# Attention in turns of six units instead of three, each turn followed at once by its own products with v

## The chip, the cores and the metric

The kernel runs on one core of a Trainium2 chip. The metric is the time of one execution on the device in microseconds, as the median of several runs. A core has a matrix engine (TensorE, "PE" in the profile; its weight loads are a row of their own, "PEld"), a vector engine (VectorE, "DVE"), a scalar engine with activation functions (ScalarE, "ACT"), a general engine (GpSimd, "POOL") and a queue engine (SyncE, "SP"). The matrix engine writes to PSUM, which here is used as eight banks of 128 partitions x 512 float32. The engines run their own instruction streams in order and wait for one another through semaphores.

## The reference

What is computed, cut to what matters. Queries and keys are each put into the cluster whose centroid they are closest to; a query attends only to keys of its own cluster. Then comes a mixture of experts, where each row goes to one expert.

```python
# q, k, v: (4 batches, 8 heads, 768 rows, 64); centroids: (8, 16, 64)
q_assign = np.argmax(einsum('bhsd,hcd->bhsc', q_n, c_n), axis=-1)     # q_n, k_n, c_n: normed
k_assign = np.argmax(einsum('bhsd,hcd->bhsc', k_n, c_n), axis=-1)
mask = q_assign[:, :, :, None] == k_assign[:, :, None, :]
scores = where(mask, q @ k.T / 8, -1e9)
attn = softmax(scores)                 # exp, divided by its sum + 1e-9
x = (attn @ v) as (3072 rows, 512)
# experts: 8, x (3072, 512), w1 (8, 512, 1024), w2 (8, 1024, 512)
expert_idx = argmax(x @ w_gate); gate_w = the softmax probability of that expert
out[row] = gate_w[row] * (relu(x[row] @ w1[e]) @ w2[e])
```

## The kernel before

Attention works on 16 groups of two heads of one batch. A group has 12 units: two halves of the queries (384 each) by six blocks of 128 keys. There are thus 192 units. One unit is scored in `score`: for each of the two heads a float32 matmul of keys by queries, then a bf16 matmul that adds the mask (a one-hot product, made so that another cluster's score becomes hugely negative). The result, two banks of PSUM ("sps"), is put through the exponential by ACT into an SBUF tile A, and DVE adds A to a running sum T. `attend` multiplies A by v and collects six units in one bank O.

```python
NB = 3                                  # units of a turn
ps_s = tile_pool(name="ps_s", bufs=NB, space=PSUM)      # three double banks "sps"
ps_o = tile_pool(name="ps_o", bufs=1, space=PSUM)       # one bank  "O"
ps_m = tile_pool(name="ps_m", bufs=1, space=PSUM)       # one bank  "mps"
def wide(): return ps_s.tile([P, 2, 512], F32, name="sps")
ap = tile_pool(name="ap", bufs=2 * NB)                  # the tiles A

def score(u):
    g, half, j = where(u)
    ps = ps_s.tile([P, 2, 512], F32, name="sps")
    for a in range(2):                                  # L673, contraction over 64 rows
        nc.tensor.matmul(ps[:, a, 0:HS], lhsT=qk[g][r, 1, ks], rhs=qk[g][r, 0, qs], start=True, stop=False)
    for a in range(2):                                  # L676, the mask
        nc.tensor.matmul(ps[:, a, 0:HS], lhsT=ohT[g][r, 1, ks], rhs=ohT[g][r, 0, qs], start=False, stop=True)
    nc.scalar.activation(A[u], ps[:, :, 0:HS], AF.Exp)  # L678
    # L681 (j == 1) and L685 (j > 1): T[g, half] += A[u] on DVE

def attend(u):                                          # L693, output of 64 partitions per head
    for a in range(2):
        nc.tensor.matmul(O[g, half][a * D : (a + 1) * D, 0:HS], lhsT=rows[g, "v"][:, a, j, :], rhs=a_[:, a, :], ...)
```

Everything else of the attention is cut into jobs that are placed between scores and products. `turn` transposes q and k of a later group (L599; DVE copies one part with the scale at L603, ACT the rest at L604 and L606). `similar` and `similar2` multiply them by the centroids and transpose the result (L613, L624). `assign` and `assign2` find the closest centroid (DVE L632, L633, POOL L634, DVE L640, L641), and `put` transposes the one-hot rows (L651; ACT L655 and DVE L656 copy them to ohT). After a group, `finish` copies O (ACT L701), `weigh` and `weigh2` make the sums and the gate's logits (L711, L725, then five small DVE operations from L727), and `x_turn` transposes the outputs (L754) and scales them on DVE (L757).

```python
def similar(g):
    ps = ps_m.tile([P, 512], F32, name="mps")
    ...                                                 # four matmuls, L613
    nc.scalar.copy(sims[g], ps[:, 0:HS])                # L618
def similar2(g):
    ps = ps_m.tile([P, 512], F32, name="mps")
    ...                                                 # three transposes, L624
    nc.scalar.copy(sims[g], ps[:, 0:HS]...)             # L626

for n in range(-4, NTURN + 5):
    for x in range(n * NB, (n + 1) * NB):               # the scores of this turn's units
        score(x)
    for f, a in jobs.get((n, 0), ()): f(*a)             # jobs, first part
    for x in range((n - 1) * NB, n * NB):               # the products of the turn before
        attend(x)
    for f, a in jobs.get((n, 1), ()): f(*a)             # jobs, second part
```

`gate` and `keep_rows` close a batch (every fourth group); `choose`, `count`, `slots1`, `one_hots1` and `tokens1` sort the first three batches' rows by expert during the last batch's attention. The experts' two layers follow (L301, L345) with gathers and scattered writes on POOL (L270, L316).

Of the kernel before, what the change touches and what calls it, by code (L numbers as in the profile page):

```python
# [8 lines left out]
F32 = mybir.dt.float32  # L9
# [5 lines left out]
PSUM = bass.MemoryType.PSUM  # L15
# [2 lines left out]


BIG = float(2**60)  # L20
NB = 3
XU = 2
RQ = 32
NP = 3
# [159 lines left out]
def kernel(  # L184
# [11 lines left out]
    nc = tc.nc  # L196
    B, H, S, D = q.shape
    C = centroids.shape[1]
    P = 128
    NQ = S // P  # L200
    HP = H // 2
    NG = B * HP
    HS = S // 2
# [6 lines left out]
    FB = F // P  # L210
# [19 lines left out]
    def fetch(e, i):  # L230
        i %= 3
        w1 = wpools[i].tile([P, DB, F], F32, name=f"w1_{i}")
        w2 = wpools[i].tile([P, FB, Dm], F32, name=f"w2_{i}")
        nc.sync.dma_start(out=w1, in_=moe_w1[bass.ds(e, 1)].rearrange("e (a p) f -> p (e a) f", p=P))
        nc.sync.dma_start(out=w2, in_=moe_w2[bass.ds(e, 1)].rearrange("e (a p) d -> p (e a) d", p=P))
        return w1, w2
# [20 lines left out]

    late = ExitStack()
    p1 = late.enter_context(tc.tile_pool(name="first", bufs=2))
    ps_s = late.enter_context(tc.tile_pool(name="ps_s", bufs=NB, space=PSUM))  # L260
    ps_o = late.enter_context(tc.tile_pool(name="ps_o", bufs=1, space=PSUM))
    ps_m = late.enter_context(tc.tile_pool(name="ps_m", bufs=1, space=PSUM))


    def wide():
        return ps_s.tile([P, 2, 512], F32, name="sps")
# [88 lines left out]
    def cols_of(t, c0):  # L355
        return lambda j: t[:, c0 + j : c0 + j + 1]
# [125 lines left out]
    def indices(pool, ps, w, gi, si):  # L482
# [14 lines left out]
            n=[P], rows=NF * P, e=e, gi=cols_of(g_idx1, e), si=cols_of(s_idx1, e), apart=True, scalar_only=True  # L497
# [5 lines left out]
    with ExitStack() as actx:  # L503
# [1 line left out]
        qkp = actx.enter_context(tc.tile_pool(name="qkp", bufs=2))  # L505
        ohp = actx.enter_context(tc.tile_pool(name="ohp", bufs=2))
        asg = actx.enter_context(tc.tile_pool(name="asg", bufs=2))
        ap = actx.enter_context(tc.tile_pool(name="ap", bufs=2 * NB))
        tp_ = actx.enter_context(tc.tile_pool(name="tsum", bufs=2))
        stat = actx.enter_context(tc.tile_pool(name="stat", bufs=2))  # L510
        xp = actx.enter_context(tc.tile_pool(name="xp", bufs=1))
# [1 line left out]
        pl = actx.enter_context(tc.tile_pool(name="places1", bufs=1))  # L513
# [75 lines left out]
        qk, sims, ohT = {}, {}, {}  # L589
# [17 lines left out]

        def similar(g):

            ps = ps_m.tile([P, 512], F32, name="mps")  # L610
            for t in range(4):
                w, half = divmod(t, 2)
                nc.tensor.matmul(  # L613
                    ps[t * 2 * C : (t + 1) * 2 * C, 0:HS], lhsT=cblk[:, g % HP].rearrange("p a c -> p (a c)"),
                    rhs=qk[g][:, w, half * HS : (half + 1) * HS], start=True, stop=True,
                )
            sims[g] = asg.tile([P, HS], F32, name="simT", bufs=1)
            nc.scalar.copy(sims[g], ps[:, 0:HS])  # L618

        def similar2(g):  # L620
            simT = sims.pop(g)
            ps = ps_m.tile([P, 512], F32, name="mps")
            for i in range(NQ // 2):
                nc.tensor.transpose(ps[:, i * P : (i + 1) * P], simT[:, i * P : (i + 1) * P], ident)  # L624
            sims[g] = asg.tile([P, G, C], F32, name="sim")
            nc.scalar.copy(sims[g], ps[:, 0:HS].rearrange("p (t c) -> p t c", c=C))  # L626
# [32 lines left out]
        A, T, O = {}, {}, {}  # L659
        X, XT = {}, {}  # L660

        def where(u):
            g, r = divmod(u, 2 * NQ)
            return g, r // NQ, r % NQ

        def score(u):
            g, half, j = where(u)
            qs = slice(half * HS, (half + 1) * HS)
            ks = slice(j * P, (j + 1) * P)
            ps = ps_s.tile([P, 2, 512], F32, name="sps")  # L670
            for a in range(2):
                r = slice(a * D, (a + 1) * D)
                nc.tensor.matmul(ps[:, a, 0:HS], lhsT=qk[g][r, 1, ks], rhs=qk[g][r, 0, qs], start=True, stop=False)  # L673
            for a in range(2):
                r = slice(a * D, (a + 1) * D)
                nc.tensor.matmul(ps[:, a, 0:HS], lhsT=ohT[g][r, 1, ks], rhs=ohT[g][r, 0, qs], start=False, stop=True)  # L676
            A[u] = ap.tile([P, 2, HS], F32, name="A")
            nc.scalar.activation(A[u], ps[:, :, 0:HS], AF.Exp)  # L678
            if j == 1:
                T[g, half] = tp_.tile([P, 2, HS], F32, name="T", bufs=4)  # L680
                nc.vector.scalar_tensor_tensor(  # L681
                    T[g, half], in0=A[u - 1], scalar=1e-9 / P, in1=A[u], op0=ALU.add, op1=ALU.add
                )
            elif j > 1:
                nc.vector.tensor_tensor(T[g, half], T[g, half], A[u], op=ALU.add)  # L685

        def attend(u):
            g, half, j = where(u)
            if j == 0:
                O[g, half] = ps_o.tile([P, 512], F32, name="O")  # L690
            a_ = A.pop(u)
            for a in range(2):
                nc.tensor.matmul(  # L693
                    O[g, half][a * D : (a + 1) * D, 0:HS], lhsT=rows[g, "v"][:, a, j, :], rhs=a_[:, a, :],
                    start=(j == 0), stop=(j == NQ - 1),
                )
# [89 lines left out]
        def at(n, part, f, *a):  # L786
            jobs.setdefault((n, part), []).append((f, a))

        UG = 2 * NQ
        NU = NG * UG  # L790
        TG = UG // NB
        TH = NQ // NB
        NTURN = NG * TG
        at(1, 1, place_consts)
        for g in range(NG):
            n = g * TG
            if g == 1:

                for f, a in ((turn, (g, 0)), (turn, (g, 1)), (similar, (g,)), (similar2, (g,))):
                    at(-1 if f is similar2 else -2, 1, f, *a)  # L800
            else:
                at(n - 4, 0, turn, g, 0)
                at(n - 4, 1, turn, g, 1)
                at(n - 3, 0, similar, g)
                at(n - 3, 1, similar2, g)
            at(n - 2, 0, assign, g)
            at(n - 2, 0, assign2, g)
            at(n - 1, 0, put, g)
            at(n + TH, 1, finish, g, 0)
            at(n + 2 * TH, 1, finish, g, 1)  # L810
            if g < NG - 1:
                at(n + TG + 2, 0, weigh, g)
                at(n + TG + 2, 1, weigh2, g)
                at(n + TG + 3, 1, x_turn, g, 0)
                at(n + TG + 4, 0, x_turn, g, 1)
                if g % HP == HP - 1:
                    at(n + TG + 3, 0, gate, g // HP)
                    at(n + TG + 4, 0, keep_rows, g // HP)


        front = parts[0]
# [35 lines left out]
            layer1(g, (f0, f1))  # L857

        n = (NG - HP) * TG
        at(n + 3, 1, choose, pl, front)  # L860
        at(n + 4, 1, count, front)
        at(n + 5, 0, slots1)
        at(n + 5, 1, one_hots1, 0)
        at(n + 6, 0, one_hots1, 1)
        at(n + 7, 0, tokens1)
        for i in range(NP):
            at(n + 7, 1, gather1, i)
            at(n + 13, i % 2, turn_rows1, i)

        n = NG * TG  # L870
        at(n + 1, 0, first_half, 0, 0, FB // 4)
        at(n + 1, 0, weigh, NG - 1)
        at(n + 1, 0, first_half, 0, FB // 4, FB // 2)
        at(n + 1, 0, weigh2, NG - 1)
        at(n + 1, 0, x_turn, NG - 1, 0)
        at(n + 1, 1, x_turn, NG - 1, 1)
        at(n + 1, 1, gate, B - 1)
        at(n + 1, 1, keep_rows, B - 1)
        at(n + 2, 0, first_half, 0, FB // 2, FB)
        for g in range(2, NG):  # L880
            at((g - 2) * TG + 1, 0, load, g)

        def early(e):
            weights[e] = fetch(e, e)

        for e in range(2):
            at(HP * TG * (e + 1) - 7, 0, early, e)

        for n in range(-4, NTURN + 5):
            for x in range(n * NB, (n + 1) * NB):  # L890
                if 0 <= x < NU:
                    score(x)
            for f, a in jobs.get((n, 0), ()):
                f(*a)
            for x in range((n - 1) * NB, n * NB):
                if 0 <= x < NU:
                    attend(x)
            for f, a in jobs.get((n, 1), ()):
                f(*a)
# [5 lines left out]
    with tc.tile_pool(name="sm", bufs=1) as sm:  # L905
        front, back = parts
# [20 lines left out]
        for part in parts:  # L927
            n, over = part["n"], part["over"]
# [85 lines left out]
    with tc.If(nx > XU):  # L1014
        with tc.For_i(XU, nx, 1) as i:
# [4 lines left out]
            g = dict(n=[P], rows=N, w=fetch(ex, 0), gi=lambda j: gi[:, 0:1], si=lambda j: gi[:, 1:2], apart=False)  # L1020
# [36 lines left out]
```

## Time and profile before

| | before |
|---|---|
| time, median of 3 runs (lowest to highest) | 864.28 us (863.96 to 864.37) |
| span of the profiled execution | 862.4 us |
| mean granted TensorE clock | 0.993 of full |
| PE / PEld / DVE / ACT / POOL busy | 97% / 50% / 36% / 31% / 12% |
| HBM read and written | 68.26 MB, 13.68 MB |
| first score to last product with v | 21.95 to 428.91 us |

The profile's page gives busy shares of each engine, then the span in 40 equal slices with a digit for tenths of busy time, then groups of instructions: source line, engine, operation, the tiles written and read, count, busy time, mean duration in ns, and the idle time of the engine just before them with what ended it. The timeline lists instructions in order of time, with neighbours of the same line merged: start, duration, engine, line, operation, form, count. A float32 matmul of the program stands as two records. The form shows the part of the array in use: 64*128 is 64 rows of contraction by 128 columns of output.

### The profile page before, as it was taken

The page shows a single profiled execution, that of the slowest core. Times are in us where ns is not written, and L with a number is a line of the kernel's source. Part 1 is how long each engine was busy: PE and PEld are TensorE (multiplying, and loading weights), DVE is VectorE, ACT ScalarE, POOL GpSimd, SP SyncE. Part 2 cuts the span into 40 slices and gives each one's busy share as a digit, 9 for nine tenths or more (in the row PEclk, how much of TensorE's full clock was granted, in tenths as well). Part 3 has the DMA queues.
Part 4 walks back from the last instruction along what each step waited for, and adds up shares of the span by engine and source line. Part 5 has one row for each costly group of instructions (what it writes and reads, how often), then busy time and mean ns, then how long its engine had stood idle before and what let it go on. Part 6 is the DMA issues. An engine that isn't in the chain of part 4 may idle for free.

```text
span 862.4 us, 10765 instructions
## 1 busy us (share of the span) xinstructions
PE 832.5 (97%) x4397; PEld 435.3 (50%) x4397; DVE 307.7 (36%) x543; ACT 271.2 (31%) x422; POOL 107.4 (12%) x165
## 2 busy tenths in 40 slices
PE   4999999999999999999999999999999999999994
PEld 3444544444445444444576646645444454545472
DVE  2655566565565665875543101010101010101000
ACT  3554544554545555544311111111111111110010
POOL 3000000000000000130004211302020303010010
PEclk8999999999999999999999999999999999999998
DMA  9025320482222122210060245434242423312010
GB/s 203 1 57 217 88 55 11 121 251 56 55 81 59 46 55 56 93 38 1 8 274 15 66 141 205 159 110 152 110 150 110 164 98 119 136 67 90 24 38 7
DMA packets 76186, 81.69 MB, mean 95 GB/s; under 512 B 52831, under 2 KB 56927, under 8 KB 75616
## 3 DMA queue, kind: packets, MB, share of 16 engines
q1 hardware_dynamic: 70208, 60.82, 23.0%
q0 software_dynamic: 5248, 20.04, 6.5%
q8 instruction: 37, 0.61, 0.3%
q14 instruction: 21, 0.17, 0.1%
q10 hardware_dynamic: 672, 0.05, 0.1%
HBM read 68.26 MB, written 13.68 MB: 95 GB/s over the span
## 4 chain that ended last, share of the span: by engine, by line
PE 46%; issue 38%; POOL 8%; DVE 5%; ACT 1%; DMA 0%; POOLq 0%; ACTq 0%; DVEq 0%
PE sps L673 14%; PE O L693 14%; PE mps L711 4%; PE sps L676 3%; POOL out_dram L316 3%; POOL xg L270 3%; PE sps L599 3%; PE sps L301 2%; PE mps L613 2%; DVE T L685 2%; PE sps L754 2%; PE sps L651 1%; POOL oh_c L468 1%; PE mps L624 1%; PE sps L345 1%
## 5 line engine op out<-in xcount | busy, mean ns | idle before, releaser
L678 ACT ACTIVATE A<-sps 128x768 f32<-128x768 f32 x192 | 154.4, 810 | 71.1 <-PE sps L676 70.0
L301 PE MATMUL sps<-xgT,w 128*128 128x416 f32 (+2 forms) x640 | 175.2, 434 | 1.1 <-ACT xgT L290 1.1
L673 PE MATMUL sps<-qk 64*128 64x384 f32 x768 | 163.7, 501 | 0.5 <-DVE x L757 0.5
L345 PE MATMUL sps<-w,h_sb 128*128 128x512 f32 x368 | 160.6, 595 | 1.3 <-DVE h_sb L309 0.9
L301 PEld LDWEIGHTS sps<-xgT,w 128*128 128x128 f32 x640 | 111.1, 190 | 67.5 <-issue 49.8
L685 DVE TENSOR_TENSOR T<-T,A 128x768 f32<-128x768 f32 x128 | 122.6, 958 | 47.6 <-ACT A L678 37.6
L693 PE MATMUL O<-A,v_in 128*64 128x384 f32 x768 | 138.0, 494 | 0.0
L309 DVE TENSOR_SCALAR h_sb<-sps 128x416 f32<-128x416 f32 (+2 forms) x34 | 18.7, 550 | 316.6 <-PE sps L301 316.6
L345 PEld LDWEIGHTS sps<-w,h_sb 128*128 128x128 f32 x368 | 69.1, 190 | 91.7 <-issue 85.6
L673 PEld LDWEIGHTS sps<-qk 64*128 64x128 f32 x768 | 68.1, 187 | 36.5 <-issue 33.7
L693 PEld LDWEIGHTS O<-A,v_in 128*64 128x64 f32 x768 | 49.4, 136 | 69.7 <-issue 68.2
L315 ACT ACTIVATE zo<-sps,xg 128x512 f32<-128x512 f32 (+1 forms) x34 | 23.3, 685 | 180.0 <-PE sps L345 171.0
L316 POOL DMA_INDIRECT out_dram<-zo,s_idx x34 | 33.0, 970 | 319.0 <-ACT zo L315 316.1
L676 PE MATMUL sps<-ohT 64*128 64x384 bf16 x384 | 66.2, 324 | 2.2 <-DVE ohT L656 2.2
L311 ACT ACTIVATE h_sb<-sps 128x416 f32<-128x416 f32 (+2 forms) x34 | 16.5, 484 | 162.8 <-DVE h_sb L309 162.8
L681 DVE SCALAR_TENSOR_TENSOR T<-A 128x768 f32<-128x768 f32 x32 | 30.7, 959 | 82.1 <-ACT A L678 82.1
L634 POOL TENSOR_TENSOR sim<-sim,first_c 128x384 f32<-128x384 f32 x16 | 16.0, 997 | 291.3 <-DVE sim L633 291.3
L270 POOL DMA_INDIRECT xg<-x_rows,g_idx x34 | 33.3, 980 | 22.8 <-issue 9.8
L676 PEld LDWEIGHTS <-ohT 64*128 64x128 bf16 x384 | 22.1, 94 | 26.5 <-DVE ohT L656 5.4
L701 ACT COPY xT<-O 128x384 f32<-128x384 f32 x32 | 15.4, 481 | 31.4 <-PE O L693 31.4
L711 PE MATMUL mps<-T,one_row 128*32 128x384 f32 x128 | 23.7, 492 | 0.0
L345 PE MATMUL sps<-w,h 128*128 128x512 f32 x48 | 21.3, 597 | 1.4 <-ACT h L311 1.4
(191 smaller groups left out, 532.2 us busy)
## 6 DMA issues: line engine op xcount, KB each, us to landing
w<-in_moe_w_dram SPq DMA_DIRECT2D x20, 2048.0 KB, 8.7
x_rows<-x POOLq DMA_DIRECT2D x4, 1548.0 KB, 7.2
q_in<-in_q_dram SPq DMA_DIRECT2D x32, 192.0 KB, 4.5
k_in<-in_k_dram SPq DMA_DIRECT2D x32, 192.0 KB, 4.6
v_in<-in_v_dram SPq DMA_DIRECT2D x16, 384.0 KB, 3.4
xg<-x_rows,g_idx POOLq DMA_INDIRECT x34, 5.1
out_dram<-zo,s_idx POOLq DMA_INDIRECT x34, 2.9
csb<-in_centroids_dram ACTq DMA_DIRECT2D x1, 32.0 KB, 1.8
```

Source lines behind the costliest of these rows:

```text
L270: nc.gpsimd.indirect_dma_start(out=g["xg"][0:m, j, :], out_offset=None, in_=x_d[0 : g["rows"], :], in_offset=bass.IndirectOffsetOnAxis(ap= ...
L301: nc.tensor.matmul(o, lhsT=g["w"][0][:, c, fb * P : (fb + 1) * P], rhs=g["xT"][:, c, :cols], start=(c == 0), stop=(c == DB - 1),)
L316: ins = nc.gpsimd.indirect_dma_start(out=out[:, :], out_offset=bass.IndirectOffsetOnAxis(ap=g["si"](j)[0:m], axis=0), in_=zo[0:m], in_offs ...
L345: nc.tensor.matmul(zp, lhsT=g["h"][:, fb, j * P : (j + 1) * P], rhs=g["w"][1][:, fb, :], start=(fb == 0), stop=(fb == FB - 1),)
L599: nc.tensor.transpose(ps[:, i * P : (i + 1) * P], rows[g, "qk"[w]][:, j].rearrange("p a d -> p (a d)"), ident)
L673: nc.tensor.matmul(ps[:, a, 0:HS], lhsT=qk[g][r, 1, ks], rhs=qk[g][r, 0, qs], start=True, stop=False)
L676: nc.tensor.matmul(ps[:, a, 0:HS], lhsT=ohT[g][r, 1, ks], rhs=ohT[g][r, 0, qs], start=False, stop=True)
L678: nc.scalar.activation(A[u], ps[:, :, 0:HS], AF.Exp)
L681: nc.vector.scalar_tensor_tensor(T[g, half], in0=A[u - 1], scalar=1e-9 / P, in1=A[u], op0=ALU.add, op1=ALU.add)
L685: nc.vector.tensor_tensor(T[g, half], T[g, half], A[u], op=ALU.add)
L693: nc.tensor.matmul(O[g, half][a * D : (a + 1) * D, 0:HS], lhsT=rows[g, "v"][:, a, j, :], rhs=a_[:, a, :], start=(j == 0), stop=(j == NQ - 1),)
L711: nc.tensor.matmul(ps[half * 32 : (half + 1) * 32, 0:HS], lhsT=one_row[:, i, :] if i < 2 else wg[:, g % HP, :], rhs=t[half][:, i, :] if i ...
```

## The change

A turn has six units instead of three, so that a group (12 units) takes two turns instead of four. The number of double banks in PSUM stays at three, so six units' scores go through them one after the other. The products with v now follow in the same turn as their scores, not in the turn after. The jobs keep their order from group to group, but have half as many places to stand in. `similar` and `similar2` take a double bank instead of the single one, and the copy after `similar` moves from ACT to DVE. There are seven tiles A instead of six, and three tiles T instead of four. The loads of q, k and v are placed anew. It is meant to let the matrix engine work longer on one kind of matmul at a time.

```diff
-NB = 3
+NB = 6
-    ps_s = late.enter_context(tc.tile_pool(name="ps_s", bufs=NB, space=PSUM))
+    ps_s = late.enter_context(tc.tile_pool(name="ps_s", bufs=3, space=PSUM))
-        ap = actx.enter_context(tc.tile_pool(name="ap", bufs=2 * NB))
+        ap = actx.enter_context(tc.tile_pool(name="ap", bufs=NB + 1))
         def similar(g):
-            ps = ps_m.tile([P, 512], F32, name="mps")
+            ps = wide()[:, 0, :]
...
-            nc.scalar.copy(sims[g], ps[:, 0:HS])
+            nc.vector.tensor_copy(sims[g], ps[:, 0:HS])
         def similar2(g):
-            ps = ps_m.tile([P, 512], F32, name="mps")
+            ps = wide()[:, 0, :]
...
-                T[g, half] = tp_.tile([P, 2, HS], F32, name="T", bufs=4)
+                T[g, half] = tp_.tile([P, 2, HS], F32, name="T", bufs=3)
...                                       # n = g * TG, TG = UG // NB: 4 before, 2 now
-                at(n - 4, 0, turn, g, 0)
-                at(n - 4, 1, turn, g, 1)
-                at(n - 3, 0, similar, g)
-                at(n - 3, 1, similar2, g)
+                at(n - 3, 0, turn, g, 0)
+                at(n - 3, 0, turn, g, 1)
+                at(n - 3, 1, similar, g)
+                at(n - 2, 0, similar2, g)
             at(n - 2, 0, assign, g)
             at(n - 2, 0, assign2, g)
             at(n - 1, 0, put, g)
-            at(n + TH, 1, finish, g, 0)
-            at(n + 2 * TH, 1, finish, g, 1)
+            at(n, 1, finish, g, 0)
+            at(n + 1, 1, finish, g, 1)
             if g < NG - 1:
-                at(n + TG + 2, 0, weigh, g)
-                at(n + TG + 2, 1, weigh2, g)
-                at(n + TG + 3, 1, x_turn, g, 0)
-                at(n + TG + 4, 0, x_turn, g, 1)
+                at(n + 2, 0, weigh, g)
+                at(n + 2, 1, weigh2, g)
+                at(n + 2, 1, x_turn, g, 0)
+                at(n + 3, 1, x_turn, g, 1)
                 if g % HP == HP - 1:
-                    at(n + TG + 3, 0, gate, g // HP)
-                    at(n + TG + 4, 0, keep_rows, g // HP)
+                    at(n + 3, 0, gate, g // HP)
+                    at(n + 3, 1, keep_rows, g // HP)
...                                       # the sorting of rows and the loads, placed anew
-            for x in range((n - 1) * NB, n * NB):
+            for x in range(n * NB, (n + 1) * NB):
                 if 0 <= x < NU:
                     attend(x)
```

More of the change, by code (lines that the diff above doesn't have):

```diff
@@ L793 @@
         NTURN = NG * TG
-        at(1, 1, place_consts)
+        at(0, 1, place_consts)
         for g in range(NG):
             n = g * TG
-            if g == 1:
+            if g == 0:
+                at(-4, 0, turn, g, 0)
+                at(-4, 1, turn, g, 1)
+                at(-3, 0, similar, g)
+                at(-3, 1, similar2, g)
+            elif g == 1:
                 for f, a in ((turn, (g, 0)), (turn, (g, 1)), (similar, (g,)), (similar2, (g,))):
@@ L859 @@
         n = (NG - HP) * TG
[L860 to L865, printed above, removed]
+        at(n + 1, 1, choose, pl, front)
+        at(n + 2, 0, count, front)
+        at(n + 2, 1, slots1)
+        at(n + 3, 0, one_hots1, 0)
+        at(n + 3, 1, one_hots1, 1)
+        at(n + 4, 1, tokens1)
         for i in range(NP):
-            at(n + 7, 1, gather1, i)
-            at(n + 13, i % 2, turn_rows1, i)
+            at(n + 4, 1, gather1, i)
+        at(n + 6, 0, turn_rows1, 0)
+        at(n + 6, 1, turn_rows1, 1)
+        at(n + 7, 0, turn_rows1, 2)
         n = NG * TG
[L871 to L879, printed above, removed]
+        at(n, 0, first_half, 0, 0, FB // 4)
+        at(n, 0, weigh, NG - 1)
+        at(n, 0, first_half, 0, FB // 4, FB // 2)
+        at(n, 0, weigh2, NG - 1)
+        at(n, 0, x_turn, NG - 1, 0)
+        at(n, 1, x_turn, NG - 1, 1)
+        at(n, 1, gate, B - 1)
+        at(n, 1, keep_rows, B - 1)
+        at(n + 1, 0, first_half, 0, FB // 2, FB)
         for g in range(2, NG):
-            at((g - 2) * TG + 1, 0, load, g)
+            at(max(g * TG - 6, -1), 1, load_qk, g)
+            at(max(g * TG - 5, -1), 1, load_v, g)
         def early(e):
@@ L886 @@
         for e in range(2):
-            at(HP * TG * (e + 1) - 7, 0, early, e)
+            at(HP * TG * (e + 1) - 4, 0, early, e)
         for n in range(-4, NTURN + 5):
```

## The prediction, made before the changed kernel was run

> **What bounds the kernel now.** I read the page first: busy shares, the slices, then the groups of the attention.
>
> ```profile
> PE 832.5 (97%) x4397; PEld 435.3 (50%) x4397; DVE 307.7 (36%) x543; ACT 271.2 (31%) x422; POOL 107.4 (12%) x165
> ...
> PE   4999999999999999999999999999999999999994
> ...
> PEclk8999999999999999999999999999999999999998
> ...
> L678 ACT ACTIVATE A<-sps 128x768 f32<-128x768 f32 x192 | 154.4, 810 | 71.1 <-PE sps L676 70.0
> ...
> L673 PE MATMUL sps<-qk 64*128 64x384 f32 x768 | 163.7, 501 | 0.5 <-DVE x L757 0.5
> ...
> L693 PE MATMUL O<-A,v_in 128*64 128x384 f32 x768 | 138.0, 494 | 0.0
> ...
> L676 PE MATMUL sps<-ohT 64*128 64x384 bf16 x384 | 66.2, 324 | 2.2 <-DVE ohT L656 2.2
> ```
>
> The matrix engine is full from the second slice on, at full clock, and waits of a fraction of a microsecond stand before the attention's matmuls: 0.5 us before the scores, 0.0 before the products with v, 2.2 before the masks. ACT is idle for 71 us before the exponentials, always for PE. So PE's own work is the bound, and only what shortens PE's stream can shorten attention. But busy is not the same as streaming at full rate, so I read the timeline of PE in one ordinary stretch (columns: start us, duration us, engine, line, operation, tiles, form, count):
>
> ```profile
> 256.64 2.16 PE L693 MATMUL O<-A,v_in 128*64 128x384 f32 x12
> 258.72 0.55 PE L624 MATMUL mps<-ident,simT 128*128 128x128 f32 x3
> 259.20 0.92 PE L673 MATMUL sps<-qk 64*128 64x384 f32 x4
> 259.95 0.33 PE L676 MATMUL sps<-ohT 64*128 64x384 bf16 x2
> 260.11 0.81 PE L673 MATMUL sps<-qk 64*128 64x384 f32 x4
> 260.76 0.33 PE L676 MATMUL sps<-ohT 64*128 64x384 bf16 x2
> 260.92 0.81 PE L673 MATMUL sps<-qk 64*128 64x384 f32 x4
> 261.56 0.33 PE L676 MATMUL sps<-ohT 64*128 64x384 bf16 x2
> 261.82 1.48 PE L711 MATMUL mps<-T,one_row 128*32 128x384 f32 x8
> ```
>
> The starts matter, not the durations. The second and third unit start 0.91 and 0.81 after the unit ahead of them (259.20, 260.11, 260.92), so a unit costs 0.805 us once the engine is in its stride. Three would be 2.415 us, yet from 259.20 to the next kind of work at 261.82 it is 2.62. A run of scores thus carries about 0.205 us that no unit needs: 0.10 at its first unit, 0.10 behind its last. In the same way the products take 2.08 us from 256.64 to 258.72; the starts of their weight loads in the trace lie 0.322 us apart in the stride, two per unit, so three units need 1.935 and the run carries 0.15 us more. These two figures repeat to a few nanoseconds in all ordinary turns.
>
> **What the Trainium skill says.** "TensorEngine Tiling (Array Packing)", section Key Properties: "Changing tiling mode (not just tile) drains the TensorE". The forms fit: scores are 64*128, products 128*64, transposes 128*128, and each border between them costs about 0.1 us in this trace. "Perfetto Trace Analysis", section Matmuls, asks that independent matmul groups rotate through PSUM banks so that evacuation of one overlaps the next; the trace agrees, see the next view. "TensorE: Matmul & The Clock Gate", section Why this matters for your kernels, warns of gaps that lower the clock; the clock row is at 9 through the whole attention, so nothing is to be won or lost there.
>
> **Six units through three double banks.** With six scores in a row the fourth needs the bank of the first, so ACT must empty banks as fast as PE fills them. The kernel before does this once, in its first two turns, where no products stand between. From the timeline of all engines:
>
> ```profile
> 23.71 0.81 PE L673 MATMUL sps<-qk 64*128 64x384 f32 x4
> 23.92 4.85 ACT L678 ACTIVATE A<-sps 128x768 f32<-128x768 f32 x6 [1.32 <-PE sps L676]
> ...
> 24.52 0.81 PE L673 MATMUL sps<-qk 64*128 64x384 f32 x4
> ...
> 26.14 0.81 PE L673 MATMUL sps<-qk 64*128 64x384 f32 x4
> ...
> 26.63 4.15 DVE L685 TENSOR_TENSOR T<-T,A 128x768 f32<-128x768 f32 x4
> ...
> 26.95 0.81 PE L673 MATMUL sps<-qk 64*128 64x384 f32 x4
> ...
> 27.85 2.16 PE L693 MATMUL O<-A,v_in 128*64 128x384 f32 x12
> ```
>
> Six exponentials take 4.85 us, 0.81 each, back to back, and PE keeps its 0.81 spacing to the sixth unit with no wait. So ACT follows at the same pace, one unit behind. The sums on DVE end at 30.78, 3 us after the last score, which the products (4 us for six units) cover.
>
> **The change part by part.** (a) Half as many runs. Scores: 64 runs become 32, saving 32 x 0.205 = 6.6 us. Products: 32 x 0.15 = 4.9 us. Together 11.5 us, all on PE and so on the path. (b) Jobs. Their count and work are the same. Standing together (all twelve transposes of `turn` in one run; L711 next to L624; L725 next to L754) they lose about one border per group, near 0.07 us x 15 = 1 us. (c) The waits of before. PE's waits between 22 and 429 us are 2.2 (masks for ohT), 0.8 (L651 for the one-hots of group 1) and 0.5 (scores for x): 3.5 us. In the new order the one-hot rows are ready a turn ahead and ohT is copied while six products run, so they should go: 3.5 us. (d) Copies after `similar` on DVE: 16 x 0.5 us of an engine that is busy for 36%; off the path, unless its queue is late. Sum of gains: 16.0 us.
>
> **New waits.** I laid the DVE queue beside PE's for the two kinds of turn, time 0 at the first score, with durations of before. Sums end at 8.0 (as above: 2.8 to the second exponential's end, then five at 1.05). In a group's second turn PE goes scores 5.0, L651 0.8, twelve L599 1.45, products 4.0 = 11.25, then L754, and L613 at 11.7. L613 needs qk complete: DVE copies ohT (0.55) and qk (0.95) after the sums, to 9.8, then ACT copies its parts (0.37 and 0.6) to 10.9: a margin of 0.8 us. In the three turns with `gate`, 1.4 us of small DVE operations go first, so qk is late by about 0.5 us: 3 x 0.5 = 1.5 us. In the turn with `one_hots1`, after `slots1` (2.4 us) and with 1.35 us for each one-hot tile, I expect 2.5 us. In a group's first turn the assignment (DVE, POOL, DVE), the five small operations after L725 and L757 end at 14.0, and the third score of the next turn, which takes that double bank, comes at 14.0: 0.1 us x 15 = 1.5 us. Sum of new waits: 5.5 us.
>
> 864.3 - 16.0 + 5.5 = 853.8, rounded to 853.5 us. The experts' half, from 429 us on, is the same and only moves ahead.
>
> **Rivals.** First: PSUM becomes the bound. Two more jobs per group (`similar`, `similar2`) draw double banks from the same rotation, so a job waits for an exponential, and a score for a job's copy. If each turn lost 0.35 us, 11 us would go and the time would be 864 us: no gain. Against it speaks the run of six above, and ACT, which is free at the start of each turn. Second: DVE becomes the bound in bursts. It has about 5.5 us of sums at the start of each turn and then the jobs' copies behind them, in order; if sums slip into the next turn, tiles A (seven) stay taken and exponentials stop. That would be 1 us per turn or more, 32 us and more, 886 us. Against it: per group DVE has some 16 us of work in 25 us. Third, to the good side: the borders may cost more than I can see, as the job runs also carry some. If every run of jobs saved 0.1 us as well, 3 us more would go: 850 us.
>
> **Range and chances.** The gain of (a) is firm, 11.5 us; (c) and the new waits are each uncertain by half and partly cancel. This gives 849.5 to 858 us for 8 in 10. For 2% the time would have to fall under 847.0, which needs all gains, no new waits and more: 5%. Slower by 2% needs the second rival: 2%. The rest, 93%, lies within 2%.
>
> **What would show it.** Right: from first score to last product about 396 us instead of 407; a run of six scores takes 5.04 us from its first start to the next kind, a run of six products 4.02 us; L678 still follows PE with 0.81 spacing. Wrong: waits of PE before L673 for ACT (first rival) or for DVE (second) of more than 6 us in all; waits of L613 for ACT's L606 in ordinary turns; or runs whose border cost doubles with their length, so that it isn't the borders that cost.

## The result, and the profile after

The changed kernel takes 851.43 us (median; 851.04 to 852.3) against 864.12 us (863.9 to 864.37) of the kernel before beside it: 12.7 us less, a ratio of 0.9854 with a 95% interval of 0.9837 to 0.9872. The profiled execution spans 849.3 us instead of 862.4.

From the page of the changed kernel, the lines that answer to those shown of before:

```profile
PE 820.6 (97%) x4397; PEld 435.6 (51%) x4397; DVE 320.5 (38%) x559; ACT 264.0 (31%) x406; POOL 106.2 (13%) x165
...
PE   4999999999999999999999999999999999999994
...
L678 ACT ACTIVATE A<-sps 128x768 f32<-128x768 f32 x192 | 153.1, 811 | 50.2 <-PE sps L676 48.9
...
L673 PE MATMUL sps<-qk 64*128 64x384 f32 x768 | 158.6, 491 | 0.0
...
L693 PE MATMUL O<-A,v_in 128*64 128x384 f32 x768 | 130.9, 490 | 0.0
...
L676 PE MATMUL sps<-ohT 64*128 64x384 bf16 x384 | 63.2, 323 | 0.3 <-DVE ohT L656 0.3
```

PE runs the same 4397 instructions, is as full as before (97%, and a 9 in nearly every slice), and yet needs 11.9 us less for them. The busy share could not have shown this gain: what went away was counted as busy. Idle time before the masks fell from 2.2 to 0.3 us. ACT waits for PE 21 us less, since it now works in longer stretches, but it still waits for PE and not the other way.

PE's timeline in one first turn of a group and the start of the next turn:

```profile
152.63 4.09 PE L693 MATMUL O<-A,v_in 128*64 128x384 f32 x24
156.65 0.40 PE L725 MATMUL mps<-ident,lsT 64*128 64x64 f32 x3
156.98 0.55 PE L754 MATMUL sps<-ident,xT 128*128 128x128 f32 x3
157.46 0.92 PE L673 MATMUL sps<-qk 64*128 64x384 f32 x4
...
158.37 0.81 PE L673 MATMUL sps<-qk 64*128 64x384 f32 x4
...
159.18 0.81 PE L673 MATMUL sps<-qk 64*128 64x384 f32 x4
159.82 0.33 PE L676 MATMUL sps<-ohT 64*128 64x384 bf16 x2
159.98 0.81 PE L673 MATMUL sps<-qk 64*128 64x384 f32 x4
...
160.79 0.81 PE L673 MATMUL sps<-qk 64*128 64x384 f32 x4
...
161.60 0.81 PE L673 MATMUL sps<-qk 64*128 64x384 f32 x4
162.24 0.33 PE L676 MATMUL sps<-ohT 64*128 64x384 bf16 x2
162.50 0.68 PE L651 MATMUL sps<-ident_b,oh 128*128 128x128 bf16 x9
```

Six products take 4.02 us from start to start (152.63 to 156.65), six scores 5.04 (157.46 to 162.50). The first gap is 0.91, all others 0.81, the fourth to sixth too: no unit waits for a double bank here. In the whole attention one unit does, by 0.3 us: the second score of the turn at 405.57, for DVE's L757. PE's waits between 22 and 420 us, as the list of waits has them (us in total, times, longest):

```profile
PE sps L613 <- DVE qk L603: 1.7, 1, 1.7
PE sps L676 <- DVE ohT L656: 0.3, 1, 0.3
```

**Where the 13.0 us of the attention came from.** First score to last product went from 406.96 to 393.93 us. The table adds up the time from the start of each run to the start of the next kind of work:

| | before | after | difference |
|---|---|---|---|
| scores | 173.2 us | 162.3 us | -10.9 |
| products with v | 133.5 us | 130.5 us | -3.0 |
| all jobs | 100.2 us | 101.1 us | +0.9 |

The two kinds of run have a part per unit and a part per run. Undisturbed runs of one to six units stand in this kernel (six) and in two of the experiments below (two and four; one and three): 1.008, 1.817, 2.624, 3.431 and 5.046 us for one, two, three, four and six scores, and 0.796, 1.441, 2.087, 2.731 and 4.022 us for as many products. Both are straight lines: 0.808 us a unit and 0.200 us a run for scores, 0.645 and 0.151 us for products. The kernel before has 63 runs of scores, not 64, since its first six units stand in one piece; so there are 31 runs fewer of scores and 32 of products, and borders gave 6.2 + 4.8 = 11.0 us. The scores' other 4.7 us are delays that went. Five runs of the kernel before were 0.84 to 1.16 us longer than undisturbed ones, behind the waits that PE's list has. Its first run took 5.90 us, against 5.52 now and 5.05 undisturbed: TensorE's granted clock was 0.50 until 23.71 us, and the scores began at 21.95; now it is 0.50 only until 20.88, before they begin. The products gained 4.8 us by borders and lost 1.8 to the new wait at L613, which stands behind one run of them. L613's own slow run there (1.57 instead of 0.78 us, it waited again, for ACT's part of qk) is most of the +0.9 in the jobs.

### The profile page after: what moved, and what is told of

The parts are those of the page before. It is cut to its first block, busy times and chain, and to the rows that moved or that the text cites. A ratio compares the mean times of both kernels' runs of the same rounds, so it can differ in the third digit from the quotient of the medians.

```text
span 849.3 us, 10767 instructions
## 1 busy us (share of the span) xinstructions
PE 820.6 (97%) x4397; PEld 435.6 (51%) x4397; DVE 320.5 (38%) x559; ACT 264.0 (31%) x406; POOL 106.2 (13%) x165
## 4 chain that ended last, share of the span: by engine, by line
PE 48%; issue 39%; POOL 8%; DVE 3%; ACT 1%; DMA 0%; POOLq 0%; ACTq 0%; DVEq 0%
PE sps L673 14%; PE O L693 14%; PE mps L711 4%; PE sps L676 3%; POOL out_dram L316 3%; POOL xg L270 3%; PE sps L599 2%; PE sps L613 2%; PE sps L754 2%; PE sps L301 2%; PE sps L651 1%; POOL oh_c L468 1%; PE sps L624 1%; PE sps L345 1%; DVE T L685 1%
## 5 line engine op out<-in xcount | busy, mean ns | idle before, releaser
L673 PE MATMUL sps<-qk 64*128 64x384 f32 x768 | 158.6, 491 | 0.0
L693 PE MATMUL O<-A,v_in 128*64 128x384 f32 x768 | 130.9, 490 | 0.0
L673 PEld LDWEIGHTS sps<-qk 64*128 64x128 f32 x768 | 66.6, 187 | 47.7 <-issue 41.2
L693 PEld LDWEIGHTS O<-A,v_in 128*64 128x64 f32 x768 | 52.3, 137 | 62.7 <-issue 62.6
L676 PE MATMUL sps<-ohT 64*128 64x384 bf16 x384 | 63.2, 323 | 0.3 <-DVE ohT L656 0.3
L676 PEld LDWEIGHTS <-ohT 64*128 64x128 bf16 x384 | 19.3, 94 | 25.5 <-DVE ohT L656 0.9
L757 DVE TENSOR_TENSOR x<-sps,rd 128x384 f32<-128x384 f32 x32 | 17.6, 553 | 28.4 <-PE sps L754 28.4
L711 PE MATMUL mps<-T,one_row 128*32 128x384 f32 x128 | 23.8, 492 | 0.0
```

What stands on the lines that cost most here:

```text
L711: nc.tensor.matmul(ps[half * 32 : (half + 1) * 32, 0:HS], lhsT=one_row[:, i, :] if i < 2 else wg[:, g % HP, :], rhs=t[half][:, i, :] if i ...
```

## Experiments

All times are medians, to be compared with 851.4 us. The kernel before took 864.3 to 864.5 us beside them.

**One cut more per turn.** Runs of scores and products double, and the jobs, buffers and order between turns stay.

```diff
-  six scores; jobs; six products; jobs
+  four scores; two products; two scores; jobs; four products; jobs
```

> The changed kernel with each turn's six scores and six products cut once more: four scores, two products, two scores, jobs, four products. Nothing else differs. If borders between kinds of matmul cost (my theory), each of 32 turns has one more run of scores (0.205 us) and one more of products (0.15 us): 851.4 + 11 = 861 to 863 us. If the gain came from products in the same turn, from jobs that stand together or from the waits that went (rival), the time stays at 851 to 853 us, since all these are kept.

Measured: 875.7 us, 24.3 more, slower than the kernel before (ratio 1.0131, 1.0114 to 1.0148). The rival, that the gain came from the order, from jobs that stand together or from waits alone, falls as the whole account, for the borders are there as expected and take back 11 of the 13 us. But 24 is not 11. The borders: 3.43 + 1.82 us for the scores and 1.44 + 2.73 for the products, 0.36 us a turn more than in one piece. The rest is mostly one wait. The timeline after a group's first turn, PE first, then DVE:

```profile
165.25 0.55 PE L754 MATMUL sps<-ident,xT 128*128 128x128 f32 x3
165.72 0.92 PE L673 MATMUL sps<-qk 64*128 64x384 f32 x4
166.47 0.33 PE L676 MATMUL sps<-ohT 64*128 64x384 bf16 x2
166.64 0.81 PE L673 MATMUL sps<-qk 64*128 64x384 f32 x4
167.28 0.33 PE L676 MATMUL sps<-ohT 64*128 64x384 bf16 x2
167.92 0.92 PE L673 MATMUL sps<-qk 64*128 64x384 f32 x4 [0.31 <-DVE x L757]
```

```profile
162.86 0.55 DVE L632 TENSOR_REDUCE mx<-sim 128x24 f32<-128x384 f32 x1 [0.98 <-ACT sim L626]
...
166.25 0.35 DVE L727 COPY ls<-mps 128x192 f32<-128x192 f32 x1
...
167.31 0.55 DVE L757 TENSOR_TENSOR x<-sps,rd 128x384 f32<-128x384 f32 x1
```

The third score needs the double bank that L754 filled, and DVE empties it only at 167.86, at the end of a chain that began with `similar2` and runs through the assignment and the small operations from L727 on. Four products hide 1.29 us less of that chain than six. In the changed kernel L757 ends at 158.71 and the third score starts at 159.18, some 0.4 us later:

```profile
158.16 0.55 DVE L757 TENSOR_TENSOR x<-sps,rd 128x384 f32<-128x384 f32 x1
```

So the cut took more than the slack: 1.29 - 0.47 = 0.82 us. Start to start, the scores behind these turns take 0.52 to 0.83 us too long in twelve groups, 9.0 us in all. PE's list of waits has only 5.8 us of it, as idle time before L673.

**Three cuts per turn.**

> The changed kernel with three more cuts per turn: three scores, one product, one score, one product, one score, one product, one score, jobs, three products. Borders theory: three times the loss of one cut, 851.4 + 3 x 10 to 11 = 881 to 885 us, in a straight line with the number of runs. Rival: 851 to 855 us.

Measured: 908.1 us, 56.7 more. Its 128 runs of each kind cost 96 x (0.200 + 0.151) = 34 us more than 32 runs, close to the 30 to 33 expected; the other 23 us are waits, again mostly for L757 (13.6 us in PE's list, 1.2 us at most, and others).

**The cut in second turns only.** This separates the two: the chain on DVE stands in first turns, which stay whole.

```diff
-  every turn: six scores; jobs; six products; jobs
+  first turn of a group: the same
+  second turn: four scores; two products; two scores; jobs; four products; jobs
```

> The changed kernel with the one cut per turn (four scores, two products, two scores, jobs, four products) in a group's second turn only. Borders theory: 16 x 0.355 us = 5.7 us, and no waits, because the chain on DVE that held the bank of the third score stands in first turns, whose products are whole here: 857.1 us. If the surplus of the cut in every turn (24 us in place of 11) was the cost of the borders themselves, half of it comes: 863.5 us.

Measured: 858.3 us, 6.9 more. Borders are 16 x 0.351 = 5.6 us of it, and the waits for L757 are gone (none in PE's list). The remaining 1.3 us is L613 in the three turns with `gate`, 1.26 us instead of 0.83, with weight loads that wait for ACT's copy of qk. Half of the full cut's 24 us, which is 12, did not come: borders cost 0.35 us a pair, the rest was waits.

**What makes a border: another form, or any interruption?** A small matmul that nobody reads goes into the middle of each run of scores, once in the scores' form, once in that of the transposes.

```diff
                     score(x)
+                    if x % NB == 2:
+                        dps = ps_m.tile([P, 512], F32, name="mps")
+                        nc.tensor.matmul(dps[:, 448:512], lhsT=ident[0:64, :], rhs=ident[0:64, 0:64], start=True, stop=True)
# the other kernel: lhsT=ident, rhs=ident[:, 0:64]
```

> The changed kernel with one small float32 matmul (64 columns, into the single bank, read by nobody) in the middle of each turn's run of scores, with 64 rows of contraction: the same form as the scores. If what costs is the change of the array's form, it costs its own streaming of about 0.11 us: 32 x 0.11 = 3.5 us, 854 to 855.5 us. If any interruption of a run costs (another bank, other weights), it costs as much as the other form: 861 us or more.

> The same small matmul with 128 rows of contraction, the form of the transposes. Change of form: its own 0.11 us and two borders of 0.1 us each, 32 x 0.31 = 10 us, 860 to 863 us. Any interruption: the same time as with 64 rows, within 1 us.

Measured: 858.4 us in the same form (+7.0), 868.35 in the other (+16.9). Timelines of PE, first the same form, then the other:

```profile
150.51 0.33 PE L676 MATMUL sps<-ohT 64*128 64x384 bf16 x2
150.68 0.22 PE L903 MATMUL mps<-ident 64*128 64x64 f32 x1
150.68 0.59 PE L673 MATMUL sps<-qk 64*128 64x384 f32 x1
150.73 0.27 PE L903 MATMUL mps<-ident 64*128 64x64 f32 x1
150.84 0.86 PE L673 MATMUL sps<-qk 64*128 64x384 f32 x3
```

```profile
153.33 0.33 PE L676 MATMUL sps<-ohT 64*128 64x384 bf16 x2
153.59 0.43 PE L903 MATMUL mps<-ident 128*128 128x64 f32 x2
153.95 0.92 PE L673 MATMUL sps<-qk 64*128 64x384 f32 x4
```

In the same form the small matmul slides between the scores, whose records even overlap it, and a turn takes 0.22 us more. In the other form the mask before it lasts 0.26 us to the next start instead of 0.16 (153.33 to 153.59), and the next score shows the long 0.92 of a first unit; a turn takes 0.57 us more. Both were expected too low (0.11 and 0.31). Streaming 64 columns is about 0.11 us, an estimate from 0.645 us for 384 columns of the products. In the same form the trace shows where twice that comes from. The unit behind the small matmul takes 0.91 us to the next, as the first unit of a run does. And the two heads' matmuls, which started 0.006 us apart before it, start 0.11 us apart from there to the end of the run, which ends that much later. The loads of the small matmul's weights take the same time in both forms (187 and 188 ns). The difference of 0.35 us (0.31 by the times of the two kernels) belongs to the change of form. It is also what one more run of scores and one more of products cost, 0.351 us. This agrees with what the Trainium skill, "TensorEngine Tiling (Array Packing)", section Key Properties, says of a change of tiling mode.

**One part of the change undone.** `similar` and `similar2` use the single bank again, and ACT copies.

```diff
-            ps = wide()[:, 0, :]                           # in similar and in similar2
+            ps = ps_m.tile([P, 512], F32, name="mps")
-            nc.vector.tensor_copy(sims[g], ps[:, 0:HS])
+            nc.scalar.copy(sims[g], ps[:, 0:HS])
```

> The changed kernel with one part undone: similar and similar2 write to the single bank again, and ACT does the copy after similar. In a group's first turn similar2 now stands right behind weigh, which uses the same bank, and waits for ACT's copy of it: 0.65 us x 14, so 860 to 862 us, with a wait of L624 for ACT L718. If the double banks for these two jobs are no help (rival: they only crowd the rotation), 850 to 851.5 us.

Measured: 861.7 us, 10.3 more. PE's waits in this kernel:

```profile
PE mps L624 <- ACT lsT L718: 8.0, 14, 0.6
PE mps L613 <- DVE qk L603: 1.6, 1, 1.6
PE mps L432 <- ACT sim L626: 0.6, 1, 0.6
```

From L711's start to L624's, these turns take 9.0 us more in all, so nearly the whole loss stands at this one place. The run puts back both jobs' bank and the copy's engine together; the wait names the bank of `similar2`. So this small part of the change protects most of its gain: with half as many places for jobs, two that use one bank come to stand side by side, and without another bank for one of them the wait would have taken 10 of the 13 us back.

**The constants earlier,** by one turn, ahead of the first scores.

```diff
-        at(0, 1, place_consts)
+        at(-1, 1, place_consts)
```

> The changed kernel with place_consts three places earlier, before the first scores, so that GpSimd makes the constants ahead of the second group's assignment, as it did in the kernel before. The wait of 1.75 us before the first L613 between turns, and its slow run (1.57 us in place of 0.78) should both go: 851.4 - 2.5 = 848.5 to 849.5 us. If that wait is hidden by something later, 851 us.

Measured: 849.3 us, 2.1 less (ratio to before 0.9828, 0.9812 to 0.9845). The wait of L613 is gone from PE's list, and its runs between turns take 0.83 us at most. In the changed kernel GpSimd made the constants behind the second group's assignment, DVE stood idle 3.67 us for one of them (L394), and the sums, ohT and qk behind it in DVE's queue all came late:

```profile
37.05 0.18 DVE L394 TENSOR_SCALAR hl_i<-tok_i 128x24 int32<-128x24 int32 x1 [3.67 <-POOL tok_i L391]
...
44.13 1.64 PE L613 MATMUL sps<-qk,cblk 128*32 128x384 f32 x8 [1.75 <-DVE qk L603]
```

**Two borders fewer per group.** The second `x_turn` moves behind `turn`'s transposes, into the single bank; the first moves ahead of `weigh2`, its scaling by DVE stays behind.

```diff
-                at(n + 2, 1, weigh2, g)
                 at(n + 2, 1, x_turn, g, 0)                 # transposes only
-                at(n + 3, 1, x_turn, g, 1)
+                at(n + 2, 1, weigh2, g)
+                at(n + 2, 1, x_scale, g, 0)                # the scaling on DVE
+            at(g * TG + 3, 0, x_turn, g, 1)                # after turn's, with its scaling
```

> The changed kernel with two borders fewer per group and no run longer: the second x_turn's transposes stand behind turn's transposes (same form, into the single bank), and the first x_turn's stand ahead of weigh2's, so that weigh2's 64-row transposes run into the scores in one form. Borders theory: 2 x 0.1 us x 15 = 3 us, 848 to 849.5 us. Rival (only runs of scores and products count): 851 to 852 us.

Measured: 856.95 us, 5.5 more: the opposite of what I expected. With the constants early as well it is 854.3 us.

> The last two edits together. If both hold and are apart from each other, their gains add: 851.4 - 2.5 - 3 = 845.5 to 846.5 us.

The gain of the constants shows in both (849.3 - 851.4 and 854.3 - 857.0), the moves lose. DVE, then PE, in a first turn of the kernel with the two moves (in its numbering L757 on PE is the transposes of `x_turn`, L765 their scaling):

```profile
159.53 0.36 DVE L727 COPY ls<-mps 128x192 f32<-128x192 f32 x1 [0.79 <-PE mps L725]
...
160.61 0.55 DVE L765 TENSOR_TENSOR x<-sps,rd 128x384 f32<-128x384 f32 x1
```

```profile
158.62 0.55 PE L757 MATMUL sps<-ident,xT 128*128 128x128 f32 x3
159.10 0.33 PE L725 MATMUL mps<-ident,lsT 64*128 64x64 f32 x2
159.22 0.59 PE L673 MATMUL sps<-qk 64*128 64x384 f32 x1
...
161.30 0.92 PE L673 MATMUL sps<-qk 64*128 64x384 f32 x4
```

L725 runs into the scores without a gap, as planned. But it comes 0.48 us later, so the chain that ends in the scaling does too (161.16), while the scores come earlier. The third score waits for its bank until 161.30, and the six scores take 5.5 us here and 5.8 in most first turns, instead of 5.05. The same 0.4 us of slack again.

**Only the move that has slack.** The constants early, and the second `x_turn` behind `turn`'s; the first stays.

> The changed kernel with the constants placed early and with only the second x_turn moved, behind turn's transposes; the first x_turn stays behind weigh2. In the run with both moves the border that went there saved 0.15 us a group, and the wait came from the other move, which put weigh2 later and the third score earlier. Theory: 849.3 - 14 x 0.15 = 847.2 us, and runs of six scores back at 5.05 us. If the move into the single bank itself causes the wait (rival): 854 us, as with both moves.

Measured: 848.2 us (847.53 to 848.64), a ratio to before of 0.981 (0.9797 to 0.9824), and no wait of PE's matmuls in its list between 22 and 420 us. The rival, that the single bank causes the wait, falls. It is 1.1 us better than with the constants alone; I expected 2.1. Compared with that kernel, the transposes L599 and L754 fell from 33.5 to 31.9 us together, but L613 rose by 0.5 us: four of its weight loads now wait for ACT's copies of qk (2.4 us in PEld's list, most of it covered).

## Why the prediction was right

**The bound and the borders (part a).** 11.5 us expected, 11.0 measured as the part per run: a run carries slightly less than I read from one stretch (0.200 us for 0.205), and I counted 64 runs of scores where the kernel before has 63. The mechanism is shown by runs: with 48 runs of each kind, where the wait for L757 does not come, the time rises as the borders say, and a change of form costs more than an interruption in the same form.

**Six units through three double banks.** Right: starts stay 0.81 us apart and L673 has 0.0 us of idle time before it. The first rival (PSUM: a score waits for a job's copy of a double bank) took 0.3 us once in the changed kernel. It was closer than I thought: with the cut in every turn it took 9 us.

**Jobs (b).** 1 us expected, nothing came: +0.1 us apart from the slow L613. L599 and L651 gained 3.5 us in all, as runs of transposes merged. L725 lost 2.2, since it no longer runs into scores of its own form but meets L754, and L754 lost 0.8, since 13 of its 29 runs had stood directly before L599. I had counted the borders that go and not those without cost that went with them. The third rival, that the runs of jobs gain too, did not come either.

**Waits of before (c).** 3.5 us expected, 4.7 measured. I took the idle times of PE's list, and start to start these waits cost more. I also read the clock row as leaving nothing to win: a 9 in a slice of 21.6 us hid the 0.50 that the first scores ran into.

**New waits.** This is the term that was mis-sized: 5.5 us expected, 2.6 measured, and at another place. In the turns with `gate` I expected 0.5 us, and L613 ran on time: in the trace ACT's last copy of qk ends at 144.22, the very moment L613 starts. I had allowed 1.8 us for DVE's copies of ohT and qk and 1.1 for ACT's; they took 1.5 and 0.9. In the turn with `one_hots1` (2.5 us expected) nothing waited, and before the third score in second turns (1.5 us expected) nothing either; the latter has 0.4 us of slack. What did wait was L613 in the first turns, for GpSimd's constants, which the prediction does not mention: it lays only the steady turns on the queues, not the start of the kernel. Beside the prediction's sum the terms are +0.5 us (a), +1.1 (b), -1.2 (c) and -2.9 (new waits): 2.5 us less in the attention, and the time is 2.4 us under the prediction's sum of 853.8. That (a) and (b) on one side and (c) on the other nearly cancel is luck.

**The second rival (DVE).** Not in the changed kernel, but close, and by another way than I thought: DVE held up PE through the double bank that L757 empties, not through tiles A. A cut that hid 1.29 us less of DVE's chain, or a move that put it 0.48 us later, brought it out.

## What to carry to other kernels

When an engine is full, measure from the start of one kind of work to the start of the next, divide by units, and look at what is left per run: it is counted as busy, and it goes with longer runs. Before jobs are moved together, list which of them share a bank, and which chain on another engine frees the bank that the next run takes: here one bank was worth 10 us, and 0.4 us of slack decided whether a change won or lost. Lay out the first turns too, not only the steady ones. Take what a wait costs from start to start: idle time in a list had 5.8 of 9.0 us.

## What the runs showed of the hardware beyond that

A border between forms is not one fixed price: the part per run is 0.200 us for scores and 0.151 for products. A run of 64-row transposes ahead of 64-row scores saved part of a border: starts of both interleave from 159.10 to 159.34 us in the last timeline, and in the kernel before L725 and three units of scores take 2.81 us together, where 0.33 us for L725 before another form and 2.62 for the scores would make 2.95.
